# Delta rule in chunks of 64 tokens instead of 128, with products in 64x64 places of the array and the order of work written by hand

## The chip, the cores and the metric

The kernel runs on one core of one Trainium2 chip. The metric is the device time of an execution in microseconds. The kernel before took 1425.95 us (median of 3 runs, 1422.16 to 1428.44).

In the profile PE is TensorE's matmul and PEld its weight load, DVE is VectorE, ACT is ScalarE, POOL is GpSimd, and SP is SyncE, which here issues most DMAs. A matmul of fp32 data leaves two records in the trace.

## What is computed

The first half is a delta rule, for 4 batches, 8 heads, 768 tokens and a head size of 48. The second half is a router with the two best of 8 experts for each of the 3072 tokens, and a mixture of experts with 384 inputs and 1024 hidden units.

```
state = 0                                     # [B, H, 48, 48]
for t in range(768):
    kt = k[t] / (norm(k[t]) + 1e-6)
    y[t]  = q[t] @ state                      # state of before the token
    v_old = kt @ state
    state = state + beta[t] * outer(kt, v[t] - v_old)

x = y as [3072, 384]
noisy = x @ w_gate + log1p(exp(x @ w_noise)) * noise
top2  = the two largest of noisy, softmax over them (+1e-9)
out   = sum over the two: weight * (relu(x @ w1[e]) @ w2[e])
```

## The kernel before

The delta rule goes through the tokens in chunks of C = 128, six of them. In a chunk, each batch is one tile of 128 tokens, with 8 heads in the free dimension, so a chunk is four tiles. Inside a chunk the dependence of tokens on one another is a triangular system, which the kernel solves with an explicit inverse.

`normalize(c)` scales the keys by their norms: squares on ACT, sums and small operations on DVE, a square root on ACT, the multiplication of `kp` on POOL. `products(c)` turns the keys (`turned`: four transposes `p_t` on PE, a copy to `kT` on ACT) and multiplies them with themselves (`gram`: `p_g`, 64-row products in two row places). ACT copies the 32x32 diagonal blocks of the result to `gd` and the rest to `at`. `invert(c)` runs on DVE: it transposes `gd` so that each of 128 partitions holds one 32x32 block (4 batches, 8 heads, 4 blocks), inverts all of them at once in 30 pairs of operations (L326, L330), and transposes back to `tb` (with `beta`) and `w32` (without). `join(c, b)` makes 64x64 inverses `w64` of pairs of them with 32x32 products `p_x` and `p_w`.

`attend(c, b)` is a generator. Its stages are: subtract what the state holds of these keys (`p_b`); the products of queries and keys, masked (`p_g`, `qk`); the upper 64 tokens' update (`solve`: `p_u`, times `beta`); their effect on the lower 64 tokens (`p_e`); the lower update; the new state (`p_s`, added on DVE to the old one in a zero padded layout `st`); the answers `p_y` from state and `qk`; their transposes `p_xt`; the router's logits `p_l`. `run(c)` takes the four batches through these stages in step. `route(c)` computes the noisy logits, the two best experts and the row of each token in its expert's buffer. Two products (`p_at`: `mask_u` with the tokens taken, `ones` with the earlier ones) count the tokens ahead. The rows are then written with indirect DMAs to `rows_x`.

The order of the main loop is `products(c+1)`, `join(c)`, `run(c)`, `route(c)`, `invert(c+1)`, the loads of `k` for chunk c+2, `normalize(c+2)`. All engines take their instructions in the order that the scheduler of the framework makes of this, and each waits by semaphores for the others. All PSUM tiles are of one pool of eight banks. After the delta rule, the mixture goes through the experts: load rows, transpose them (`p_xt`, L604), two products (L611, L620), store. At the end the two rows of each token are gathered and added.

Of the kernel before, what the change touches and what calls it, by code (L numbers as in the profile page):

```python
# [15 lines left out]
C = 128  # L16
DP = 64
Q = 32
# [5 lines left out]
def kernel(  # L24
# [30 lines left out]

    nc = tc.nc
# [6 lines left out]
    NB = C // Q  # L63
    NP = H // 2
    BH = B * H
# [6 lines left out]
    psum = ctx.enter_context(  # L72
        tc.tile_pool(name="psum", bufs=8, space=bass.MemoryType.PSUM)
    )

    def ps(shape, name):
        return psum.tile(shape, FP32, name=name, tag="ps")
# [11 lines left out]
    )  # L89

# [47 lines left out]
    def load_router():  # L138
# [8 lines left out]
        nc.sync.dma_start(  # L147
            out=noise, in_=moe_noise.rearrange("(t p) e -> p t e", p=128)
        )
# [25 lines left out]
    def deltanet(ictx):  # L175

        beta_t = const.tile([128, NCH, BH], FP32, name="beta_t")
        beta_b = const.tile([128, NCH, Q], FP32, name="beta_b")
        with tc.tile_pool(name="setup", bufs=1) as setup:
            beta_sb = setup.tile([BH, S], FP32, name="beta_sb")  # L180
            nc.sync.dma_start(out=beta_sb, in_=beta.rearrange("b h s -> (b h) s"))
            p_bt = ps([128, NCH, BH], "p_bt")
            for c in range(NCH):
                nc.tensor.transpose(
                    p_bt[:, c], beta_sb[:, c * C : (c + 1) * C], ident[0:BH, 0:BH]
                )
            nc.scalar.copy(beta_t, p_bt)
        by_block = beta.rearrange("b h (c n j) -> n (b h) c j", n=NB, j=Q)
        for n in range(NB):
            nc.sync.dma_start(out=beta_b[n * BH : (n + 1) * BH], in_=by_block[n])  # L190

        pool = ictx.enter_context(tc.tile_pool(name="att", bufs=1))

        def sb(shape, name, bufs, tag=None):
            return pool.tile(shape, FP32, name=name, tag=tag or name, bufs=bufs)

        def preset(shape, name, n, where):

            made = []
            for i in range(n):  # L200
# [6 lines left out]
        kps = preset([128, H, DP], "kp", 2 * B, lambda t: [t[:, :, D:DP]])  # L207
        qps = preset([128, H, DP], "qp", B, lambda t: [t[:, :, D:DP]])
        w64s = preset(
            [128, H, 2 * Q], "w64_", 6,  # L210
            lambda t: [t[Q : 2 * Q, :, 0:Q], t[3 * Q :, :, 0:Q]],
        )
        states = [
            preset(
                [128, NP, 2 * D], f"st{b}_", 2,
                lambda t: [t[0:DP, :, D:], t[DP:, :, 0:D]],
            )
            for b in range(B)
        ]

        group = {}
        chunk = {}
        logits = {}
        ys = {}

        def load(c, b, name):
            n = c * B + b
            src = {"k": k, "q": q, "v": v}[name]
            if name == "v":
                to = t = sb([128, H, D], "v", B + 1)  # L230
            else:
                tiles = {"k": kps, "q": qps}[name]
                t = tiles[n % len(tiles)]
                to = t[:, :, 0:D]
            nc.sync.dma_start(
                out=to, in_=src[b, :, c * C : (c + 1) * C, :].rearrange("h p d -> p h d")
            )
            group.setdefault((c, b), {})[name] = t

        def normalize(c):  # L240

            ss = sb([128, BH], "ss", 1)
            for b in range(B):
                ksq = sb([128, H, D], "ksq", 1)
                nc.scalar.activation(ksq, group[c, b]["k"][:, :, 0:D], ACTF.Square)
                nc.vector.tensor_reduce(
                    out=ss[:, b * H : (b + 1) * H], in_=ksq, axis=AX.X, op=ALU.add
                )
            root, rec, ksc = (sb([128, BH], x, 1) for x in ("root", "rec", "ksc"))
            nc.scalar.sqrt(root, ss)  # L250
            nc.vector.tensor_scalar_max(rec, root, 1e-30)
            nc.vector.reciprocal(rec, rec)
# [6 lines left out]
            for b in range(B):  # L259
                kp = group[c, b]["k"]  # L260
                nc.gpsimd.tensor_tensor(  # L261
                    out=kp[:, :, 0:D], in0=kp[:, :, 0:D],
                    in1=ksc[:, b * H : (b + 1) * H, None].to_broadcast([128, H, D]),
# [3 lines left out]
        def turned(src, name, bufs):  # L267

            p_t = ps([128, NP, 128], "p_t")
# [6 lines left out]
        def gram(lhsT, rhs):  # L276

            p_g = [ps([128, NP, 128], f"p_g{par}") for par in range(2)]
            for j in range(NP):
                for par in range(2):  # L280
                    lo = DP * par
                    nc.tensor.matmul(  # L282
                        p_g[par][:, j], lhsT[lo : lo + DP, j], rhs[lo : lo + DP, j]
                    )
            return p_g

        def products(c):
# [4 lines left out]
            gd = chunk[c, "gd"] = sb([128, Q, BH], "gd", 1)  # L292
            for b in range(B):
                g = group[c, b]
                g["kT"] = turned(g["k"], "kT", 2 * B)
                at = g["at"] = sb([128, H, C - Q], "at", 2 * B)
                for par, p in enumerate(gram(g["kT"], g["kT"])):
                    for n in range(NB):
                        rows = slice(n * Q, (n + 1) * Q)
# [71 lines left out]
        def attend(c, b):  # L371
# [15 lines left out]
            if c + 1 < NCH:  # L387
                load(c + 1, b, "q")
# [343 lines left out]
```

## Time and profile before

| | |
|---|---|
| median of 3 runs | 1425.95 us (1422.16 to 1428.44) |
| profiled execution | 1410.04 us, its span 1408.0 us |
| mean granted TensorE clock | 0.779 of full speed |
| PE busy | 1064.6 us (76%) |
| PEld busy | 771.4 us (55%) |
| DVE busy | 393.6 us (28%) |
| ACT busy | 345.3 us (25%) |
| POOL busy | 141.5 us (10%) |
| first product of the mixture | 729.13 us |

The delta rule with the router fills the first 729 us of the span, the mixture with its gather the rest. The shares of the whole span mix both halves, so the first half has to be read in windows. The granted clock is the speed that TensorE was given, as a share of 2.4 GHz: 1.00 is 2.4 GHz, 0.50 is 1.2 GHz. A row of the timeline joins neighbouring instructions of one form; its brackets hold the idle time ahead of them and the engine whose work ended it.

### The profile page before, as it was taken

The numbers are of one execution on the slowest core, as the hardware profiler recorded it, in microseconds if no ns is written. First come the engines' busy times: TensorE is split into PE (matmuls) and PEld (weight loads), VectorE is DVE, ScalarE is ACT, GpSimd is POOL, SyncE is SP. The second block draws the span as 40 slices with busy tenths as digits, with TensorE's granted clock in tenths as the row PEclk, the third lists the DMA queues.
The fourth block names the chain that finished last, engine by engine and source line by source line (L and its number), as shares of the span: only waits on it lengthen the run. The fifth ranks groups of instructions, "written<-read, shape, count | busy, mean of one in ns | idle before, by whom it ended". The sixth has DMA issues, their size and how long they took to land. (4 is left out here: it accounts for less than half of the span.)

```text
span 1408.0 us, 16439 instructions
## 1 busy us (share of the span) xinstructions
PE 1064.6 (76%) x6752; PEld 771.4 (55%) x6752; DVE 393.6 (28%) x1033; ACT 345.3 (25%) x780; POOL 141.5 (10%) x182
## 2 busy tenths in 40 slices
PE   2479259538937937959729999999999999999800
PEld 1369248527927927948725655555555555555400
DVE  1674416605545545533110100101010101010122
ACT  3650551443163164140202020201011110102022
POOL 5000210030040030020010000000000000000075
PEclk9555557756756756756559999999999999999955
DMA  8926924211211211010070122222131312000076
GB/s 219 366 74 188 369 74 126 39 45 24 46 45 24 46 46 22 20 46 1 4 248 33 63 73 79 90 73 95 67 101 61 107 56 73 12 29 6 36 205 198
DMA packets 141043, 124.15 MB, mean 88 GB/s; under 512 B 83072, under 2 KB 133248, under 8 KB 140960
## 3 DMA queue, kind: packets, MB, share of 16 engines
q1 hardware_dynamic: 134816, 104.14, 23.4%
q0 software_dynamic: 6144, 18.88, 4.4%
q8 instruction: 55, 0.90, 0.3%
q14 instruction: 28, 0.23, 0.1%
HBM read 60.09 MB, written 62.91 MB: 87 GB/s over the span
## 5 line engine op out<-in xcount | busy, mean ns | idle before, releaser
L611 PE MATMUL p_h<-xe,w1e 128*128 128x448 f32 x768 | 290.7, 540 | 1.5 <-DVE xe L605 1.5
L620 PE MATMUL p_o<-w2e,hT 128*128 128x384 f32 x896 | 290.3, 486 | 0.0
L620 PEld LDWEIGHTS p_o<-w2e,hT 128*128 128x128 f32 x896 | 170.2, 190 | 119.6 <-issue 3.0
L611 PEld LDWEIGHTS p_h<-xe,w1e 128*128 128x128 f32 x768 | 145.3, 190 | 142.9 <-issue 139.7
L615 ACT ACTIVATE hT<-p_h 128x448 f32<-128x448 f32 x128 | 69.6, 544 | 527.6 <-PE p_h L611 527.6
L624 DVE COPY yr<-p_o 128x384 f32<-128x384 f32 x56 | 31.2, 558 | 543.0 <-PE p_o L620 543.0
L687 POOL DMA_INDIRECT got<-rows_y,slot x48 | 46.8, 975 | 640.6 <-PEq L658 625.6
L282 PE MATMUL p_g<-kT 64*128 64x128 f32 x384 | 49.8, 437 | 67.3 <-ACT kT L273 67.3
L282 PEld LDWEIGHTS p_g<-kT 64*128 64x128 f32 x384 | 42.7, 324 | 76.3 <-ACT kT L273 76.3
L300 ACT COPY gd<-p_g 32x128 f32<-32x128 f32 x192 | 70.2, 365 | 50.7 <-PE p_g L282 49.0
L402 PE MATMUL p_u<-v,w 64*64 64x48 f32 x768 | 69.9, 270 | 0.0
L402 PEld LDWEIGHTS p_u<-v,w 64*64 64x64 f32 x768 | 68.1, 188 | 0.8 <-issue 0.2
L545 PE MATMUL p_at<-r_taken,mask_u 128*128 128x32 f32 x12 | 3.6, 397 | 79.0 <-DVE gate L565 61.7
L330 DVE TENSOR_TENSOR t<-t,step 128x30 f32<-128x30 f32 (+9 forms) x180 | 59.6, 331 | 5.5
L163 POOL DMA_INDIRECT rows_x<-y,slot x48 | 46.6, 971 | 143.5 <-issue 100.6
L271 PE MATMUL p_t<-ident,kp 128*128 128x128 f32 x96 | 26.7, 434 | 44.9 <-POOL kp L261 44.9
L326 DVE TENSOR_TENSOR step<-t 128x30 f32<-128x30 f32 (+9 forms) x180 | 59.2, 329 | 4.9
L453 ACT COPY y<-p_y 128x384 f32<-128x384 f32 x24 | 11.5, 479 | 196.4 <-PE p_y L447 196.4
L447 PE MATMUL p_y<-u,qk 128*128 128x48 f32 x384 | 58.6, 319 | 0.0
L447 PEld LDWEIGHTS p_y<-u,qk 128*128 128x128 f32 x384 | 57.7, 239 | 0.1
L368 PE MATMUL p_w<-w,x 32*32 32x32 f32 x768 | 41.7, 237 | 13.8 <-ACT x L363 13.6
L362 PE MATMUL p_x<-tb,at 32*32 32x32 f32 x768 | 42.8, 237 | 10.4 <-DVE tb L341 6.7
(126 smaller groups left out, 1037.9 us busy)
## 6 DMA issues: line engine op xcount, KB each, us to landing
rows_y<-zero SPq DMA_DIRECT2D x8, 3264.0 KB
w1e<-in_moe_w_dram SPq DMA_DIRECT2D x8, 1536.0 KB
w2e<-in_moe_w_dram SPq DMA_DIRECT2D x8, 1536.0 KB
rows_x<-zero SPq DMA_DIRECT2D x8, 1344.0 KB
xr<-rows_x SPq DMA_DIRECT2D x8, 1344.0 KB
rows_y<-yr SPq DMA_DIRECT2D x56, 192.0 KB
kp<-in_k_dram SPq DMA_DIRECT2D x24, 192.0 KB
qp<-in_q_dram SPq DMA_DIRECT2D x24, 192.0 KB
```

Of the source, the lines that this page charges most:

```text
L163: d = nc.gpsimd.indirect_dma_start(out=rows_x, out_offset=bass.IndirectOffsetOnAxis(ap=slot, axis=0), in_=rows, in_offset=None,).ins
L282: nc.tensor.matmul(p_g[par][:, j], lhsT[lo : lo + DP, j], rhs[lo : lo + DP, j])
L300: nc.scalar.copy(gd[rows].rearrange("p i h -> p h i")[:, b * H + par : (b + 1) * H : 2], p[rows, :, rows],)
L326: nc.vector.tensor_tensor(out=step, in0=t[:, j + 1 :, j, None].to_broadcast(shape), in1=t[:, None, j, 0:j].to_broadcast(shape), op=ALU.mult,)
L330: nc.vector.tensor_tensor(out=t[:, j + 1 :, 0:j], in0=t[:, j + 1 :, 0:j], in1=step, op=ALU.add)
L362: nc.tensor.matmul(p_x[dn, h], at[up, h, up], tb[up, b * H + h])
L402: nc.tensor.matmul(p_u[half, h], w64[half, h], r[half, h])
L447: nc.tensor.matmul(p_y[:, h], qk[:, h], u[:, h], start=(st is None and h == 0), stop=(h == H - 1), skip_group_check=True,)
L611: nc.tensor.matmul(p_h, w1e[:, do, fo * 128 : (fo + 1) * 128], xe[:, do, cols], start=(do == 0), stop=(do == KT - 1),)
L615: nc.scalar.activation(hT[:, fo, cols], p_h, ACTF.Relu)
L620: nc.tensor.matmul(p_o, hT[:, fo, i * 128 : (i + 1) * 128], w2e[:, fo], start=(fo == 0), stop=(fo == FT - 1),)
L687: nc.gpsimd.indirect_dma_start(out=g, out_offset=None, in_=rows_y, in_offset=bass.IndirectOffsetOnAxis(ap=slot[:, n : n + 1], axis=0),)
```

## The change

A chunk is now 64 tokens, twelve of them. A tile holds one chunk of two batches on its 128 partitions (a unit), so a chunk has two units, and four units in two chunks make a step. The block inverses are made for a whole step at once, as before for four tiles, the rest chunk by chunk. Since a 64x64 inverse now covers the chunk, `p_e` and the second `solve` go. `beta` is folded into `w64` by way of `tt`, so `u` is one copy on ACT. Products of keys, queries and states are 64x64, over four quadrants of the array in turns (`by_token`, and `p_s`), each into a tile of two PSUM banks (`banks`, three of them; the rest go to `bank`, two of them). `p_u` and `p_y` use two diagonal quadrants in turns, `p_x` and `p_w` two 32x32 places. A state is added on DVE in one operation to a compact `st`, and POOL copies it to the padded `wide` for `p_y`. The norm's root is an Ln and an Exp, so that ACT keeps one table of functions for the whole stage. Each load of a tile is two DMAs, `k` is loaded three steps ahead, `q` and `v` two chunks ahead, `beta_b` on ACT's queue.

The main loop sets the order by hand. `recur(c)` holds the three stages of the chain (subtract, update, state); between them `take` draws from lists of other work: answers of the chunk before, the router of the step before, products of the step after next, parts of the next step's inverse, query products of the next chunk, and joins of the next step.

```diff
-C = 128
+C = 64
+        def by_token(out, lhsT, rhs, opens=True):
+            for j in range(NP):
+                for b in range(2):
+                    for z in range(2):
+                        nc.tensor.matmul(
+                            out[rows_of[b], z, j], lhsT[rows_of[z], j, rows_of[b]],
+                            rhs(rows_of[z], j, b), start=(j == 0), stop=(j == NP - 1),
+                            skip_group_check=True,
                         )
...
+            p_k = banks(C, "p_k")
+            by_token(p_k, kT, lambda z, j, b: kT[z, j, rows_of[b]])
+            at = g["at"] = sb([128, 2, NP, Q], "at", 3 * US - NU)
+            for b in range(2):
+                for n in range(2):
+                    rows = slice(b * C + n * Q, b * C + (n + 1) * Q)
+                    nc.scalar.copy(gd[rows], p_k[rows, :, :, n * Q : (n + 1) * Q])
+                    if n == 0:
+                        nc.scalar.copy(at[rows], p_k[rows, :, :, Q:C])
...
+            nc.vector.transpose(
+                out=tt.rearrange("p i h -> p (i h)"),
+                in_=scaled.rearrange("p i j -> p (i j)"),
+            )
...
+        def within(n):
+            g = unit[n]
+            qT = g["qT"] = turned(g["q"], "qT", 2 * NU)
+            if n + 2 * NU < NCH * NU:
+                load(n + 2 * NU, "q")
+            yield
+            p_q = banks(C, "p_q")
+            by_token(p_q, g["kT"], lambda z, j, b: qT[z, j, rows_of[b]])
...
+        def recur(c):
+            units = range(c * NU, (c + 1) * NU)
+            for n in units:
+                g = unit[n]
+                st = g["st"] = states.get((c, n % NU))
+                if st is not None:
+                    p_b = banks(D, "p_b")
+                    by_token(p_b, g["kT"], lambda z, j, b: st[z, b, j])
+                    r = by_parity(g["v"])
+                    nc.vector.tensor_tensor(out=r, in0=r, in1=p_b, op=ALU.subtract)
+            yield
...
+                u = g["u"] = sb([128, H, D], "u", 2 * NU + 1)
+                nc.scalar.copy(u, p_u)
...
+                p_s = banks(D, "p_s")
...
+                new = states[c + 1, n % NU] = sb([128, 2, NP, D], f"st{n % NU}", 3)
...
+                    nc.vector.tensor_tensor(out=new, in0=p_s, in1=st, op=ALU.add)
+                wide = wides[n % NU][(c + 1) % 2]
+                for z, rows in enumerate(rows_of):
+                    nc.gpsimd.tensor_copy(wide[rows, :, :, z * D : (z + 1) * D], new[rows])
+            yield
...
+        def take(work, share):
+            for _ in range(share):
+                while work and next(work[0], work) is work:
+                    work.pop(0)
...
         for c in range(NCH):
+            s = c // 2
+            if c % 2 == 0:
+                inverse = [invert(s + 1)] if s + 1 < NS else []
+                take(inverse, 1)
+                if s + 2 < NS:
+                    normalize(s + 2)
+            answers = [answer(n) for n in range((c - 1) * NU, c * NU) if n >= 0]
+            if c % 2 == 0 and c:
+                answers.append(route_later(s - 1))
...
+            for i, _ in enumerate(recur(c)):
+                if i == 0:
+                    take(answers, 3)
+                    if grams:
+                        products(grams[0])
+                    take(inverse, 6)
...
+                else:
+                    take(nexts, 9)
+                    take(answers, 9)
+                    take(inverse, 99 if c % 2 else 5)
+                    if c % 2:
+                        take(joins, 99)
```

The change moves instructions on every engine. The first place is on PE, around the two products `p_at` of a router. Before, they stand between the last logits of a chunk and the transposes of the next keys:

```order
L459 MATMUL p_xt<-ident,y 128x128 x12
L467 MATMUL p_l<-wgn,xT 128x16 x12
L545 MATMUL p_at<-r_taken,mask_u 128x32
L271 MATMUL p_t<-ident,kp_130 128x128 x4
L546 MATMUL p_at<-r_earlier,ones 128x32
```

In the changed kernel they stand in an even chunk, between its updates `p_u` and its states `p_s`:

```order
L485 MATMUL p_u<-v,w_5_163 64x48 x16
L451 MATMUL p_xt<-ident,y 128x128 x3
L459 MATMUL p_xt<-wgn,xT 128x16 x3
L583 MATMUL p_at<-r_taken,mask_u 128x32
L297 MATMUL p_t<-ident,kp_118 128x128 x4
L584 MATMUL p_at<-r_earlier,ones 128x32
L297 MATMUL p_t<-ident,qp_144 128x128 x3
L307 MATMUL p_k<-kT 64x64 x16
L503 MATMUL p_s<-u,kp_124 64x48 x16
L503 MATMUL p_s<-u,kp_126 64x48 x16
```

The logits of the row L459 are written to the spare columns of the tile `p_xt`. The router has moved from the end of a chunk into the middle of the chain of the one after it, ahead of the state's products in the queue.

The second place is on DVE, in the recurrence. Before, pairs of the inversion (`step`, `t`) stand between the operations of four batches:

```order
L391 TENSOR_TENSOR qk<-p_g_1743,mask_u 128x4x128
L403 TENSOR_TENSOR u<-p_u,beta_t 64x384 x2
L326 TENSOR_TENSOR step<-t 128x228
L403 TENSOR_TENSOR u<-p_u,beta_t 64x384 x2
L413 TENSOR_TENSOR v<-v,p_e 64x384 x4
L403 TENSOR_TENSOR u<-p_u,beta_t 64x384 x4
L433 TENSOR_TENSOR st_0_172<-p_s,st_1_175 64x4x48 x2
```

In the changed kernel a step begins, in DVE's queue, with the router's last operations, the even chunk's states, the odd chunk's subtractions and states, and the next inversion's start:

```order
L589 TENSOR_REDUCE r_row<-r_mine 128x4
L590 CAST slot_102<-r_row 128x4
L512 TENSOR_TENSOR st_2080<-p_s,st_1435 128x384
L512 TENSOR_TENSOR st_2101<-p_s,st_1456 128x384
L419 TENSOR_TENSOR qk<-p_q,mask 128x512 x2
L477 TENSOR_TENSOR v<-v,p_b 128x2x4x48 x2
L512 TENSOR_TENSOR st_2446<-p_s,st_2080 128x384
L343 STREAM_TRANSPOSE t<-gd 128x1024
L512 TENSOR_TENSOR st_2467<-p_s,st_2101 128x384
L347 TENSOR_TENSOR t<-t,low_b 128x1024
```

The operations `u` times `beta` and `v` minus `p_e` are gone. The states of an even chunk now stand behind the whole router of the step before, and ahead of that behind the rest of an inversion.

## Rows read from the trace of the kernel before

**Rows 1.** Windows: us, then busy time (count) of each engine, clock, DMA.

```profile
core 0: us, PE busy (x) PEld busy (x) DVE busy (x) ACT busy (x) POOL busy (x), PEclk, DMA share, GB/s
296.20:319.50 23.30, 12.45 (x80) 10.00 (x80) 0.00 (x0) 13.34 (x34) 2.32 (x3) 0.50 0.01 3
319.50:334.30 14.80, 12.10 (x258) 11.85 (x256) 6.95 (x18) 9.31 (x25) 0.00 (x0) 0.50 0.01 2
334.30:386.50 52.20, 49.50 (x502) 47.75 (x500) 30.84 (x72) 8.49 (x21) 0.00 (x0) 0.77 0.23 47
...
729.00:1331.00 602.00, 600.29 (x1834) 336.78 (x1834) 57.52 (x112) 69.64 (x128) 0.00 (x0) 1.00 0.19 65
```

**Rows 2.** Timeline of PE (start us, us, engine, line, operation, tiles), router's end.

```profile
402.03 0.61 PE L545 MATMUL p_at<-r_taken,mask_u 128*128 128x32 f32 x2 [15.51 <-DVE gate L565]
```

**Rows 3.** Timeline of PE, products of each form at their places in the program.

```profile
106.53 6.74 PE L402 MATMUL p_u<-v,w 64*64 64x48 f32 x61
...
126.39 3.65 PE L427 MATMUL p_s<-u,kp 128*64 128x48 f32 x64
...
334.30 7.00 PE L381 MATMUL p_b<-st,kT 128*128 128x96 f32 x32
...
402.45 1.09 PE L271 MATMUL p_t<-ident,kp 128*128 128x128 f32 x4
...
432.29 0.24 PE L368 MATMUL p_w<-w,x 32*32 32x32 f32 x1
...
432.43 1.54 PE L362 MATMUL p_x<-tb,at 32*32 32x32 f32 x29
...
441.24 6.47 PE L381 MATMUL p_b<-st,kT 128*128 128x96 f32 x32
...
687.55 5.14 PE L467 MATMUL p_l<-wgn,xT 128*128 128x16 f32 x24
...
729.13 2.16 PE L604 MATMUL p_xt<-ident,xr 128*128 128x128 f32 x9 [28.66 <-DMA xr<-rows_x]
```

**Rows 4.** Window inside the recurrence, columns as in rows 1.

```profile
356.00:370.00 14.00, 14.00 (x157) 13.91 (x156) 5.52 (x12) 0.00 (x0) 0.00 (x0) 0.50 0.22 44
```

**Rows 5.** Groups by line: shape, count, busy us, mean ns, idle before, releaser.

```profile
L300 ACT COPY gd<-p_g 32x128 f32<-32x128 f32 x192 | 70.2, 365 | 50.7 <-PE p_g L282 49.0
L355 ACT COPY w<-w 32x256 f32<-32x256 f32 x96 | 38.6, 402 | 17.0 <-DVE r_w L493 7.4 <-DVE r_d L506 5.6 <-DVE r_w L505 1.8
...
L246 DVE TENSOR_REDUCE ss<-ksq 128x8 f32<-128x384 f32 x24 | 13.2, 551 | 40.0 <-ACT ksq L245 39.7
```

**Rows 6.** Timeline of DVE: inversions, first state, router with and without POOL.

```profile
48.91 1.25 DVE L317 STREAM_TRANSPOSE t<-gd 128x1024 f32<-128x1024 f32 x1 [3.73 <-ACT gd L300]
...
54.97 0.33 DVE L326 TENSOR_TENSOR step<-t 128x168 f32<-128x168 f32 x1
...
78.18 1.19 DVE L317 STREAM_TRANSPOSE t<-gd 128x1024 f32<-128x1024 f32 x1
...
127.53 3.29 DVE L431 COPY st<-p_s 64x192 f32<-64x192 f32 x8 [0.47 <-PE p_s L427]
...
397.41 2.23 DVE L493 TENSOR_TENSOR r_a_hit<-r_noisy,r_a_top 128x32 f32<-128x32 f32 x1
...
692.93 0.18 DVE L504 TENSOR_SCALAR r_z_pos<-logits 128x32 f32<-128x32 f32 x1 [27.81 <-ACT logits L472]
...
701.69 0.17 DVE L553 CAST slot<-r_row 128x4 int32<-128x4 f32 x1
```

**Rows 7.** Timelines of POOL (key scaling) and of SP (DMA issues).

```profile
21.35 3.19 POOL L261 TENSOR_TENSOR kp<-kp,ksc 128x384 f32<-128x384 f32 x4 [3.19 <-issue]
...
369.00 3.32 SPq L235 DMA_DIRECT2D kp<-in_k_dram  x4
```

**Rows 8.** Timeline of the weight loads, after a key product's turn.

```profile
300.03 0.72 PEld L271 LDWEIGHTS p_t<-ident,kp 128*128 128x128 f32 x4 [0.22 <-issue]
```

More of the change, by code (lines that the diff above doesn't have):

```diff
@@ L89 @@
     )
+    mask = const.tile([128, C], FP32, name="mask")
+    for lo in (0, C):
+        nc.vector.tensor_copy(mask[lo : lo + C], mask_u[lo : lo + C, lo : lo + C])
     low = const.tile([128, Q, Q], FP32, name="low")
@@ L318, in invert @@
                 out=t.rearrange("p i j -> p (i j)"),
[L319 removed]
+                in_=step[s, "gd"].rearrange("p i h -> p (i h)"),
             )
@@ L415, in attend @@
             )
             yield
-            solve(lower)
-            if c + 1 < NCH:
-                load(c + 1, b, "v")
-            yield
-            if c < NCH - 1:
-                p_s = ps([128, NP, D], "p_s")
-                for h in range(H):
-                    to = slice(h % 2 * DP, h % 2 * DP + DP)
-                    nc.tensor.matmul(p_s[to, h // 2], kp[:, h], u[:, h])
-                new = states[b][(c + 1) % 2]
-                for to, cols in ((upper, slice(0, D)), (lower, slice(D, 2 * D))):
-                    if st is None:
-                        nc.vector.tensor_copy(new[to, :, cols], p_s[to])
-                    else:
-                        nc.vector.tensor_tensor(
-                            out=new[to, :, cols], in0=p_s[to], in1=st[to, :, cols],
-                            op=ALU.add,
-                        )
@@ L452, in attend @@
-            y = sb([128, H, D], "y", B + 1)
-            nc.scalar.copy(y, p_y)
-            yield
-            y_f = y.rearrange("p h d -> p (h d)")
-            p_xt = ps([128, KT, 128], "p_xt")
-            for t in range(KT):
-                nc.tensor.transpose(p_xt[:, t], y_f[:, t * 128 : (t + 1) * 128], ident)
-            xT = sb([128, KT, 128], "xT", 2)
-            nc.scalar.copy(xT, p_xt)
-            yield
-            wgn = router["wgn"]
-            p_l = ps([128, 2, E], "p_l")
+            p_l = p_xt[:, KT * 128 : KT * 128 + 2 * E].rearrange("p (x e) -> p x e", e=E)
@@ L466, in attend @@
             for do in range(KT):
                 nc.tensor.matmul(
-                    p_l, xT[:, do], wgn[:, do], start=(do == 0), stop=(do == KT - 1)
-                )
-            if b == 0:
-                logits[c] = sb([128, B, 2, E], "logits", 1)
-            nc.scalar.copy(logits[c][:, b], p_l)
-            ys[c * B + b] = y_f
-        def run(c):
-            todo = [attend(c, b) for b in range(B)]
-            while todo:
-                todo = [a for a in todo if next(a, a) is None]
@@ L573, in deltanet, with now @@
             cleared.append(clear(rows_x, e * N, e * N + TILES * 128))
+        for n in range(2 * US, 3 * US):
+            load(n, "k")
         first_weights = load_weights(w_even, 0)
+        def now(work):
+            for _ in work:
+                pass
         normalize(0)
-        products(0)
-        invert(0)
+        for n in range(US):
+            products(n)
+        now(invert(0))
         normalize(1)
-        for c in range(NCH):
-            if c + 1 < NCH:
-                products(c + 1)
-            for b in range(B):
-                join(c, b)
-            run(c)
-            route(c)
-            if c + 1 < NCH:
-                invert(c + 1)
-            if c + 2 < NCH:
-                for b in range(B):
-                    load(c + 2, b, "k")
-                normalize(c + 2)
+        for n in range(US, 2 * US):
+            products(n)
@@ L592, in deltanet @@
+        now(answer(NU * NCH - 2))
+        now(answer(NU * NCH - 1))
+        route(NS - 1)
         return first_weights
```

438 lines of the change are left out of this document (242 added, 196 removed).

## The prediction, made before the changed kernel was run

> **What bounds the kernel now.** I read the windows first, then PE's timeline with what ended each idle time, then DVE's, then the groups by line. The mixture runs from 729.13 us [rows 3] to the end with PE busy 600.29 of 602 us [rows 1], and the change leaves its code and its data alone. So the gain or loss must come from the 729 us ahead of it. There the period of a chunk of 128 tokens (four tiles) is 441.24 - 334.30 = 107 us, from the first `p_b` of one chunk to that of the next [rows 3]. It has four stretches. The recurrence, 52.2 us, is PE's: busy 49.5 [rows 1]. Then PE waits 15.51 us, because `p_at` of the router stands ahead of everything else in its queue and DVE first ends the inversion and the router [rows 2]. Then the products, about 24 us, are ACT's: in 23.3 us PE is busy 12.45 and DVE not at all [rows 1], while ACT makes the 365 ns copies of L300, 192 of them in all [rows 5]. Last comes the join, 14.8 us, where PE and ACT work on 32x32 pieces [rows 1]. Two engines rest in each stretch while one works, and nothing of the next chunk fills the gap.
>
> **Prices of PE.** An fp32 matmul leaves two records. At the lower clock level (granted 0.50, that is 1.2 GHz) a 64x64 product in one place costs 6.74/61 = 0.110 us a record, and in two places in turn (`p_s`) 3.65/64 = 0.057 [rows 3]. A 32x32 product in one place costs 1.54/29 = 0.053, and where `p_x` and `p_w` alternate between two places five starts lie in 432.43 - 432.29 = 0.14 us, 0.028 each [rows 3]. A turn costs about half for each place added. Four 64x64 places in turn are not in the trace. The floor is the 0.028 of the smaller pair, the ceiling of a gain is no gain over two places, 0.057. I take 0.030, because rows of one family halve twice. A burst of 16 such matmuls (32 records) is then 1.0 us, between 0.9 and 1.8. On the clock: from 356 to 370 us PE is busy 14.00 of 14 us in single-place 64x64 products and the grant is 0.50 [rows 4], so such work does not hold the upper level, and I price all of it at 0.50.
>
> **The change part by part.** A step is now two chunks of 64 tokens, again four tiles; a tile holds 64 tokens of two batches. I follow the two waits that close a step.
>
> Stretch A runs from the first subtraction of `p_b` in an even chunk to the new state of that chunk. By the new order DVE holds there, ahead of that state's add, the rest of one inversion, one normalization and the router of the step before. The inversion's rest took 78.18 - 54.97 = 23.2 us [rows 6]; one of its two transposes now has the plain form that took 1.25 [rows 6], so 22.5. Two subtractions and four reductions of 128x384 at 0.55 [rows 5]: 3.3. Six small operations at 0.18 to 0.35: 1.5. The router alone took 701.69 + 0.17 - 692.93 = 8.9 [rows 6]. One operation of 0.19 stretched to 2.23 beside POOL [rows 6]: 2. After `p_at` the queue of PE holds two sets of transposes, one `p_k` and two `p_s` before the state, about 5.5 us, of which DVE's own slots cover 2: 3 more. A = 41 us. PE's own work there is some 18 us, so its price does not show; the wait of `p_at` stays, with `p_t`, `p_k` and `p_s` queued behind it.
>
> Stretch B, from that state to the next even chunk's subtraction, is PE's. Eleven bursts in four places (four `p_q`, three `p_b`, two `p_k`, two `p_s`): 11.0. Two `p_u` in two diagonal places, 32 records at 0.057: 3.6. Two `p_y`, the same plus 16 records of 96 columns, about 3.1 each: 6.2. Transposes, 5.3 sets at 1.09 less 0.2 of overlap [rows 3]: 4.8. Two `p_xt`, three transposes each instead of four: 1.3. Two of `p_l`, each six records at 5.14/24 = 0.214 [rows 3]: 2.6. The six bursts of `p_x` and `p_w` at 32 x 0.028: 5.3. Sum 34.8, and one to two us of waits for ACT's copies: B = 36. A step is 77 us against 107.
>
> What goes with it at no cost of its own: `p_e` and the second `p_u` (they were in the 52.2 us, and B no longer holds them); the multiplications by `beta`, which are folded into `tt`; the reloads of ACT's tables. ACT has 8.8 us a tile: six copies of `p_k` and four of `tt` of 32x256 at 0.40 [rows 5], and eleven more. Four tiles are 35 us, covered by 77. If that cover were gone (step under 40), ACT would be the bound. POOL gains two copies of a state for each tile, at most 0.9 each (four 128x384 multiplies took 3.19 [rows 7]); only `p_y` reads them, a stage later. SP issues twice as many loads, 24 a step at 3.32/4 = 0.83 [rows 7]: 20 us of 77, asked for one to three steps ahead; past that slack a late `k` would hold up `normalize`. The half loads move the same bytes; their price lies between nothing and those 20 us once, and I take nothing.
>
> The start: the first scaled `k` came at 21.35 [rows 7]; without the transposes of `beta` and the table loads ahead of it I read about 16. The first inversion started at 48.91 [rows 6] after four batches of 32 copies; 24 copies of 0.40 end near 32. Add 29.3 for an inversion (48.91 to 78.18 [rows 6]) and the first `tb` is there near 62 to 65, `p_u` near 82 behind join and `q` products, and the first state near 104 with the second inversion before it on DVE, against 127.53 [rows 6].
>
> The end: after the state of chunk 8 one B without `p_k`, 34; chunk 10 without an inversion, 20; chunk 11 and its answers, 28. From the last `p_l`, 687.55 + 5.14 = 692.69, to the mixture's first `p_xt` at 729.13 is 36.4 [rows 3], and from there to the span's end 1408.0 - 729.13 = 678.9; both stay. Around the span lie 2.0.
>
> Sum: 104 + 4 x 77 - 4 (no normalization in one step) + 34 + 20 + 28 + 36.4 + 678.9 + 2 = 1207. In general 863 + 4A + 5B. The profiled execution took 1410.04, the median of the runs 1425.95, a factor of 1.0113. So 1207 stands for 1221 us; I say 1220.
>
> Where PE went from `p_w` (32x32) to `p_b` (128x128), the new matmuls start at 334.30 [rows 3] with no wait named, and after a transpose's turn the weights' idle time was 0.22 [rows 8]. The Trainium skill, page "TensorEngine Tiling (Array Packing)", section "Key Properties", says that a change of the tiling mode, not of the place alone, drains TensorE. B has some 23 changes of place size: by the rule at 0.22 each, an estimate, 5 us a step and 1246 us in all; by the trace nothing. The measured rows decide for the sum; the other figure lies inside the forecast's own range below and gets no chance apart.
>
> **The rivals.** *B at the upper clock.* The recurrence's mean grant was 0.77, not 0.50 [rows 1], so part of it ran at 2.4 GHz, and denser work could hold that. PE's prices of B would fall by some 30 per cent net of ACT's waits: B = 26, 863 + 164 + 130 = 1157, 1170 us. Against it: the low grant at a full PE [rows 4]. The Trainium skill, page "TensorE: Matmul & The Clock Gate", section "Wait — 56ns, not 53.3ns?", has a gap of about 2.5 ns above the columns' time that the clock does not shorten; no row here separates it.
>
> *Four places give no more than two.* The bursts cost 1.8, eleven of them 9 us more, with waits B = 46: 863 + 164 + 230 = 1257, 1271 us. A longer A of 52, from more POOL interference, gives nearly the same. For it: only pairs have been seen. Against: 0.028 in 32x32.
>
> *The order does not bind.* Engines wait for one another as before and a step stays 107 us: 104 + 428 - 4 + 82 + 717 = 1327, 1342 us. For it: the `p_at` wait is still queued ahead of PE's work.
>
> *Slower: places run one after another.* If four places are done in series at 0.110, a burst is 3.5 instead of 1.0; eleven add 28, `p_u`, `p_y`, `p_x` and `p_w` some 14: B = 78, and start and end gain 35: 863 + 35 + 164 + 390 = 1452, 1468 us. It decides from B = 70 on, which is where 898 + 164 + 5B reaches 1410. Against it: the `p_s` and `p_x`/`p_w` rows.
>
> **How the numbers follow.** Forecast 0.56 (its own range 1185 to 1255), upper clock 0.20, two places 0.15, order not binding 0.05, series 0.04. The runs of the kernel before spread by 0.4 per cent, so 0.5 is about what a measurement can tell from no change. Only the last rival is slower: 0.04. Faster 0.95, the rest 0.01 within. The range takes in the first three and part of the fourth, 1140 to 1295.
>
> **What would show it.** In the changed profile: a step's length, from one even chunk's state to the next, of 77 us; in A, DVE without a gap and PE waiting for DVE at `p_at`; in B, PE busy above nine tenths and DVE mostly waiting for it; a burst `p_q` or `p_b` of 16 matmuls lasting 1.0 us at a grant of 0.50; the first state at 104; the mixture's first `p_xt` near 526 and 679 us from there to the end. I am wrong if a burst takes over 1.8, if ACT, POOL or a load ends PE's long waits, if the grant in B is near 1.0, or if the stretch behind the last `p_l` is not 36.

## The result, and the profile after

The changed kernel takes 1271.53 us (median of four runs, 1264.72 to 1275.98) against 1424.06 us for the kernel before (four runs): a ratio of 0.8938, 95% interval 0.8866 to 0.9009. The forecast was 1220 with a range of 1140 to 1295, so the side and the range hold; the time is 52 us over the forecast and above the forecast's own 1185 to 1255. The profiled execution took 1273.34 us with a span of 1271.6; in its terms the forecast was 1207, and the 66 us between are what has to be found. (The factor of 1.0113 between a profiled execution and the median did not come again, so the medians show the miss 14 us too small.) Every ratio in this document, and every time of the kernel before that stands beside an experiment, leaves out runs that were slower at a lower granted clock.

The first view is DVE's timeline of the changed kernel (start, length, what ended the idle time before). It gives the moments at which the states of chunks 0, 2, 4, 6 and 10 are written, the marks by which the forecast counted, and two waits of the step between.

```profile
125.31 1.02 DVE L510 COPY st<-p_s 128x384 f32<-128x384 f32 x2 [11.30 <-PE p_s L503]
...
209.02 1.02 DVE L512 TENSOR_TENSOR st<-p_s,st 128x384 f32<-128x384 f32 x2 [11.25 <-remote]
...
291.66 0.56 DVE L512 TENSOR_TENSOR st<-p_s,st 128x384 f32<-128x384 f32 x1 [9.78 <-remote]
...
338.33 0.55 DVE L271 TENSOR_REDUCE ss<-ksq 128x8 f32<-128x384 f32 x1 [4.71 <-ACT ksq L270]
...
365.26 0.17 DVE L598 TENSOR_SCALAR gate<-gate 128x4 f32<-128x4 f32 x1 [2.13 <-ACT gate L597]
...
378.59 0.56 DVE L512 TENSOR_TENSOR st<-p_s,st 128x384 f32<-128x384 f32 x1 [9.74 <-remote]
...
502.67 0.56 DVE L512 TENSOR_TENSOR st<-p_s,st 128x384 f32<-128x384 f32 x1 [0.22 <-PE p_s L503]
```

With PE's rows below, the balance against the forecast is (us):

| stretch | forecast | measured | more |
|---|---|---|---|
| start to the first state | 104 | 125.3 | +21 |
| three full steps, chunk 0 to 6 | 231 | 83.7 + 82.6 + 86.9 = 253.3 | +22 |
| chunk 6 to chunk 10 | 73 + 34 + 20 = 127 | 124.1 | -3 |
| chunk 10 to the end of the last `p_l` | 28 | 553.25 - 502.67 = 50.6 | +23 |
| to the mixture's first `p_xt` | 36.4 | 588.45 - 553.25 = 35.2 | -1 |
| from there to the span's end | 678.9 | 1271.6 - 588.45 = 683.2 | +4 |

In each full step DVE stands idle 9.7 to 11.3 us ahead of the state, until `p_s` is there; the sum had 3. PE's timeline shows why; these are its rows in one step, then at the start and at the end. `p_l` has the line's name `p_xt<-wgn,xT` here.

```profile
115.03 1.11 PE L297 MATMUL p_t<-ident,kp 128*128 128x128 f32 x4 [23.71 <-POOL kp L287]
116.08 0.98 PE L485 MATMUL p_u<-v,w 64*64 64x48 f32 x13
...
278.70 0.61 PE L583 MATMUL p_at<-r_taken,mask_u 128*128 128x32 f32 x2 [11.38 <-DVE gate L531]
...
282.08 1.32 PE L503 MATMUL p_s<-u,kp 64*64 64x48 f32 x24
283.64 0.48 PE L503 MATMUL p_s<-u,kp 64*64 64x48 f32 x6 [0.24 <-issue]
284.37 0.49 PE L503 MATMUL p_s<-u,kp 64*64 64x48 f32 x5 [0.24 <-issue]
...
287.29 0.46 PE L503 MATMUL p_s<-u,kp 64*64 64x48 f32 x4 [0.95 <-issue]
288.71 0.47 PE L503 MATMUL p_s<-u,kp 64*64 64x48 f32 x5 [0.96 <-issue]
...
293.25 0.24 PE L503 MATMUL p_s<-u,kp 64*64 64x48 f32 x1 [1.21 <-issue]
293.42 1.75 PE L297 MATMUL p_t<-ident,qp 128*128 128x128 f32 x7
295.10 1.99 PE L307 MATMUL p_q<-qT,kT 64*64 64x64 f32 x64
296.86 1.90 PE L307 MATMUL p_b<-st,kT 64*64 64x48 f32 x64
...
316.23 1.18 PE L307 MATMUL p_q<-qT,kT 64*64 64x64 f32 x64 [1.39 <-ACT qT L299]
...
519.80 0.47 PE L307 MATMUL p_b<-st,kT 64*64 64x48 f32 x4 [0.96 <-issue]
...
551.78 1.47 PE L459 MATMUL p_xt<-wgn,xT 128*128 128x16 f32 x6 [0.62 <-ACT xT L453]
...
588.45 4.49 PE L702 MATMUL p_xt<-ident,xr 128*128 128x128 f32 x21 [27.93 <-DMA xr<-rows_x]
```

The 64 records of `p_q` and of `p_b` run in one piece, 1.99 and 1.90 us. The 64 of `p_s` take from 282.08 to 293.49, in groups of some five with pauses that have no releaser ("issue"). In chunks 8 and 10 it is `p_b` that pauses in this way (the row at 519.80 is one). POOL's timeline has the eight row writes of the step at the same time:

```profile
281.64 1.04 POOL L170 DMA_INDIRECT rows_x<-y,slot  x1 [7.54 <-DVE r_mine L531]
...
290.64 0.97 POOL L170 DMA_INDIRECT rows_x<-y,slot  x1 [0.30 <-issue]
```

The windows (columns as in rows 1) show the full step from chunk 2 to chunk 4, the stretch B behind chunk 4, a burst, and the end from chunk 10 on:

```profile
core 0: us, PE busy (x) PEld busy (x) DVE busy (x) ACT busy (x) POOL busy (x), PEclk, DMA share, GB/s
209.00:291.60 82.60, 53.22 (x1163) 45.85 (x1162) 45.95 (x128) 41.01 (x90) 18.88 (x22) 0.64 0.43 128
...
291.66:323.10 31.44, 25.43 (x758) 22.32 (x760) 12.43 (x26) 16.92 (x39) 4.97 (x8) 0.88 0.69 192
...
295.10:296.80 1.70, 1.70 (x65) 1.70 (x68) 0.50 (x1) 0.59 (x1) 0.14 (x1) 0.50 0.48 96
...
502.70:553.00 50.30, 37.24 (x460) 31.08 (x452) 10.84 (x46) 6.98 (x18) 9.75 (x12) 0.50 0.09 32
```

Last, the groups by line (count, busy us, mean ns, idle before) that answer to [rows 5]:

```profile
L387 ACT COPY w<-tt 32x256 f32<-32x256 f32 x96 | 60.1, 626 | 9.5 <-DVE tt L369 8.2
L330 ACT COPY gd<-p_k 32x256 f32<-32x256 f32 x96 | 56.3, 586 | 25.0 <-PE p_k L307 14.4 <-remote 6.1 <-PE p_s L503 3.6
L503 PE MATMUL p_s<-u,kp 64*64 64x48 f32 x704 | 30.8, 284 | 15.2 <-issue 15.1
```

### The profile page after: what moved, and what is told of

It is laid out like the page before. It is cut to its first block, busy times and chain, and to the rows that moved or that the text cites. A ratio compares the mean times of both kernels' runs of the same rounds, so it can differ in the third digit from the quotient of the medians.

```text
span 1271.6 us, 20241 instructions
## 1 busy us (share of the span) xinstructions
PE 936.2 (74%) x8634; PEld 628.1 (49%) x8634; DVE 341.6 (27%) x923; ACT 332.5 (26%) x693; POOL 168.7 (13%) x222
## 5 line engine op out<-in xcount | busy, mean ns | idle before, releaser
L353 DVE TENSOR_TENSOR part<-t 128x30 f32<-128x30 f32 (+9 forms) x180 | 64.1, 356 | 4.7
L357 DVE TENSOR_TENSOR t<-t,part 128x30 f32<-128x30 f32 (+9 forms) x180 | 63.8, 354 | 4.8
L330 ACT COPY gd<-p_k 32x256 f32<-32x256 f32 x96 | 56.3, 586 | 25.0 <-PE p_k L307 14.4
L387 ACT COPY w<-tt 32x256 f32<-32x256 f32 x96 | 60.1, 626 | 9.5 <-DVE tt L369 8.2
L515 POOL COPY wide<-st 64x384 f32<-64x384 f32 x44 | 26.3, 599 | 172.2 <-DVE st L512 136.2
L702 PE MATMUL p_xt<-ident,xr 128*128 128x128 f32 x168 | 21.7, 290 | 27.9 <-DMA xr<-rows_x 27.9
L503 PE MATMUL p_s<-u,kp 64*64 64x48 f32 x704 | 30.8, 284 | 15.2 <-issue 15.1
L440 PE MATMUL p_y<-u,qk 64*64 64x48 f32 x768 | 40.2, 274 | 0.0
L307 PE MATMUL p_b<-st,kT 64*64 64x48 f32 x704 | 31.2, 283 | 12.0 <-issue 11.9
L440 PEld LDWEIGHTS p_y<-u,qk 64*64 64x64 f32 x768 | 36.5, 189 | 4.5 <-issue 3.7
```

Of the source, the lines that this page charges most:

```text
L307: nc.tensor.matmul(out[rows_of[b], z, j], lhsT[rows_of[z], j, rows_of[b]], rhs(rows_of[z], j, b), start=(j == 0), stop=(j == NP - 1), skip ...
L330: nc.scalar.copy(gd[rows], p_k[rows, :, :, n * Q : (n + 1) * Q])
L353: nc.vector.tensor_tensor(out=part, in0=t[:, j + 1 :, j, None].to_broadcast(shape), in1=t[:, None, j, 0:j].to_broadcast(shape), op=ALU.mult,)
L357: nc.vector.tensor_tensor(out=t[:, j + 1 :, 0:j], in0=t[:, j + 1 :, 0:j], in1=part, op=ALU.add)
L387: nc.scalar.copy(w64[rows, :, cols], tt[rows])
L440: nc.tensor.matmul(p_y[b, h], qk[b, h % 2, h // 2], u[b, h], start=(c == 0 and h == 0), stop=(h == H - 1), skip_group_check=True,)
```

## Experiments

Ratios are against the kernel before, measured beside the experiment on the same chip. Experiments 1 to 4 ran on one chip (kernel before 1407.55 us), 5 to 8 on a second (1413.74), 9 to 11 on a third (1397.00) and 12 on a fourth (1398.04); the two pairs turned out to differ in the pauses.

**1. Places one after another.** In `by_token` and in the loops of `p_s` the place becomes the outer loop:

```diff
-for j in range(NP):
-    for b in range(2):
-        for z in range(2):
+for b in range(2):
+    for z in range(2):
+        for j in range(NP):
```

> The 64x64 products p_k, p_q, p_b and p_s do the four of one place after another instead of going round the four places; nothing else changes. Theory (the gain of these products comes from places overlapping in turns): a burst of 32 records rises from about 1.0 us to 3.5 us at a grant of 0.50, as the one-place products of the kernel before at 0.110 us a record; 92 bursts in all, of which those beside DVE's inversion cost nothing, so 100 to 190 us more than the changed kernel, 1370 to 1460 us. Rival (a burst is bound by the supply of instructions or by weight loads, not by the place): within 20 us of 1272.

Measured 1336.64 us, ratio 0.9477 (0.9412 to 0.9542): 65 us more than the changed kernel, 76 by the ratios, and less than the 100 to 190 expected. Taking places in turns is a part of the gain, but a smaller one than was priced. The rest of the 152 us gained belongs to the shorter chunk and the order by hand, and no run takes these two apart. Sixty-one records of `p_q` took 3.83 us, 0.063 each:

```profile
333.46 3.83 PE L307 MATMUL p_q<-qT,kT 64*64 64x64 f32 x61
```

That is twice the 0.031 in turns, not the 0.110 of the single place before [rows 3]. The grant was 0.58 from 333.4 to 337.3 us, which accounts for a part; the rest is open.

**2. No row writes** (but for the last step's):

```diff
 for slot in slots:
-    spread(ys[n], slot[:, n : n + 1])
+    if s == NS - 1:
+        spread(ys[n], slot[:, n : n + 1])
```

> The rows of the first five steps are not written to rows_x (that part of the computation is left out; the last step's rows are written). Theory (PE's stalls of 0.25 to 1.2 us between groups of four to six products in the even chunks are caused by the eight indirect row writes that run at that time): the stalls go, the p_s of an even chunk take 2 us instead of 9 to 11, and the first p_xt of the mixture comes 30 to 40 us earlier, at about 550 to 558 instead of 588; time about 1235. Rival (the stalls belong to these products' place in the program, or to other transfers): the gaps stay and the time is 1265 to 1275.

Measured 1215.71 us in one run, which has no interval, beyond either figure. PE's timeline has the same `p_s` in one piece, and the windows of the last chunks have another clock:

```profile
278.89 1.91 PE L503 MATMUL p_s<-u,kp 64*64 64x48 f32 x64
```

```profile
core 0: us, PE busy (x) PEld busy (x) DVE busy (x) ACT busy (x) POOL busy (x), PEclk, DMA share, GB/s
...
460.60:497.00 36.40, 23.61 (x460) 20.10 (x452) 13.60 (x62) 8.06 (x23) 2.01 (x4) 0.76 0.01 1
```

The states of chunks 0, 6 and 10 come at 125.42, 356.41 and 460.62 us, the last `p_l` ends at 493.24 and `p_xt` starts at 528.86. So the three steps lose 253.3 - 231.0 = 22 us, chunks 6 to 10 lose 20, the end loses 50.6 - 32.6 = 18: 60 us in all, with the start unchanged. These two profiles are not of one chip; experiment 4, on the chip of this run and with the pauses in its `p_s`, took 47 us more than this run. At the end the grant was 0.76 here and 0.50 with the writes.

**3. Products behind the state.** The set of `products` (with `p_t<-ident,kp`) moves from the first half of a step to the second:

```diff
-if grams:
-    products(grams[0])
...
 take(answers, 9)
+for n in grams:
+    products(n)
```

> The key products of the step after next stand behind the state's products of the chunk in the written order, not ahead of its updates. Theory (PE's queue position: the transposes of kp wait for normalize on DVE and POOL, and p_u is queued behind them): the first state comes near 101 us instead of 125, and PE's waits for kp of 4.7, 6.1 and 8.4 us in the steps go; at least 24 us and up to 60 less, 1210 to 1247. Rival (DVE's serial work of about 40 us sets the step wherever PE's products stand): only the start gains, the steps stay at 83 to 87 us, 1245 to 1252.

Measured 1264.57 us, ratio 0.8975 (0.8898 to 0.9052): no difference from the changed kernel, and beyond either figure. The first state came at 93.62 us instead of 125.31, so the 23.71 us wait for POOL was the start's cost. But from chunk 0 to chunk 10 it took 77.3 + 84.7 + 81.5 + 81.3 + 74.6 = 399.4 us instead of 377.4: the inversion ends later, and DVE has it ahead of the odd chunk's subtraction, which then still waits for PE:

```profile
290.36 0.56 DVE L477 TENSOR_TENSOR v<-v,p_b 128x384 f32<-128x384 f32 x1 [2.77 <-PE p_b L307]
```

The inversion's last transpose stands ahead of it from 285.57 us on, and its `p_b` starts only at 289.24 on PE, behind the moved `p_k`, which now pause beside the row writes (273.0 to 282.9). Of the 31.7 us that the early start gained, 22.0 were given back by chunk 10.

**4. Inversion held** behind the chain's last DVE operation, by an added dependence:

```diff
-nc.vector.tensor_tensor(
+behind(nc.vector.tensor_tensor(
     out=part, in0=t[:, j + 1 :, j, None].to_broadcast(shape),
```

> Each part of the next step's inversion is tied behind the last subtraction or state of the chain that the program's text puts ahead of it, so that DVE cannot run ahead with it; key products stay where they are. Theory (DVE's order costs: the scheduler gathers all 30 pairs of an inversion in the even chunk ahead of the state): 13 to 20 us of the pairs move into the odd chunk where DVE waited for PE, each full step falls from 84 to about 68, time 1205 to 1235. Rival (PE's queue: p_u waits for normalize behind the transposes of kp, so the pairs only change places with other waits): within 15 us of 1272.

Measured 1262.99 us, ratio 0.8956 (0.8881 to 0.9031): no change, as the rival had it. The pairs did move: 12 stand between subtraction and state where the changed kernel has 24. The first state came at 106.41 us, 19 earlier, and 11 of these were given back by chunk 10 (388.4 us for 377.4). DVE's order alone is not what lengthens a step.

**5. Rows written a step late**, behind the even chunk's subtraction, with two more buffers for `y`:

```diff
-for n in range(s * US, (s + 1) * US):
-    for slot in slots:
-        spread(ys[n], slot[:, n : n + 1])
...
+if c % 2 == 0 and s >= 2:
+    write_rows(s - 2)
```

> The eight indirect row writes of a step are issued one step later, in the next even chunk behind its subtractions, where PE waits for DVE's inversion and for kp; all rows are still written. Theory (row writes cost by stalling PE's products that run at that time, and nothing where PE waits anyway): the stalls leave p_s and p_b, and most of the 58 us that went without the writes comes back: 1215 to 1240 us. Rival (the cost is POOL's time: its scaling of kp and its state copies stand behind the writes in its queue): the writes now stand ahead of kp's scaling, each of three full steps stays at 83 to 90 us, 1260 to 1280 us.

Measured 1250.65 us, ratio 0.8832 (0.8796 to 0.8869): a small gain at most, as the intervals just touch, and outside both figures. On PE's timeline `p_s` is whole again, and the pauses have gone with the writes to the products that now run beside them:

```profile
362.25 1.90 PE L507 MATMUL p_s<-u,kp 64*64 64x48 f32 x64
...
509.17 0.32 PE L489 MATMUL p_u<-v,w 64*64 64x48 f32 x4 [1.10 <-issue]
512.03 0.46 PE L489 MATMUL p_u<-v,w 64*64 64x48 f32 x4 [1.10 <-issue]
```

Experiment 8, on the same chip and with the writes where the changed kernel has them, has the pauses in `p_s`:

```profile
292.45 0.48 PE L503 MATMUL p_s<-u,kp 64*64 64x48 f32 x5 [0.96 <-issue]
```

So on this chip the pauses follow the writes and not the instruction. Joined with experiment 3 and with experiment 4, this version gave no more:

**6. Held, rows late, products late** (the edits of 3, 4 and 5).

> Three moves together: the inversion's parts tied to the chain's stages (as in the run with the inversion held), key products behind the state, and row writes in the next even chunk. Theory (three waits are in parallel in the chain, and taking away one leaves the next one): what none of the first two did alone shows when all are taken away; first state near 94 us, a step of 62 to 70 us, time 1160 to 1195. Rival (DVE's total work and its router ahead of the odd subtraction set the step): steps of 75 us and over, 1200 to 1235.

**7. Products late, rows late** (the edits of 3 and 5).

> Key products behind the state, and row writes in the next even chunk; the inversion is left to the scheduler. Theory (the gains of the start, 32 us, and of the stalls, 58 us, add, less the 20 that the last steps gave back): 1185 to 1210. Rival (DVE's inversion ahead of the odd subtraction takes what the writes give): 1225 to 1250.

Measured 1257.12 (0.8861 to 0.8928) and 1252.74 (0.8824 to 0.8888). Both theories that gave the order of the step the rest of the loss fell, and both rivals had lower times too (1200 to 1235, and 1225 to 1250).

**8. One store for each tile** of the output instead of two halves:

```diff
-for i in range(2):
-    t0 = (2 * u + i) * S + c * C
-    nc.sync.dma_start(out=out[t0 : t0 + C, :], in_=got[0][i * C : i * C + C])
+rows = out.rearrange("(u i s) d -> u i s d", i=2, s=S)[u, :, c * C : (c + 1) * C]
+nc.sync.dma_start(out=rows, in_=got[0])
```

> The output of a tile is stored with one DMA of 128 rows again, not with two of 64. Theory (the gather at the end, 81.5 us from the last product to the span's end instead of 77.1, pays for 24 more issues on SP): 4 us less, 1266 to 1269. Rival (the difference is the gather's own spread from run to run): within 1.5 us of the changed kernel.

Measured 1317.95 us, ratio 0.9317 (0.9286 to 0.9348): some 50 us slower, the opposite of what was expected. In SP's queue the 24 stores to three-dimensional views take 109.14 us from the first to the last, and the 48 half stores of the changed kernel 66.90:

```profile
1204.10 109.14 SPq L797 DMA_DIRECT2D out_dram<-got  x24
```

```profile
1201.36 66.90 SPq L798 DMA_DIRECT2D out_dram<-got  x48
```

The gathers on POOL tell why. They wait 52.3 us, in 18 waits, for a store to land and free its tile (us in total, times, longest); in the changed kernel it is 0.6 us:

```profile
POOL got L783 <- DMA out_dram<-got: 52.3, 18, 4.9
```

While one of these stores is under way (1268.99 to 1271.2 us) SP's queue keeps 13.5% of the 16 DMA engines busy, which is about two of them; with the half stores it is 60.7% (1241 to 1243 us). So this form of store is slow in itself, and the run says nothing of what 24 fewer issues are worth: the 4 us of the last stretch stay open.

**9. Rows in PE's waits.** Each step's writes go behind `scaled` of a later inversion, the last ones behind `z_pos` of the next router, where PE waits for DVE:

```diff
+if s >= 3:
+    write_rows(s - 3, made)
...
+if s >= NS - 2:
+    write_rows(s - 1, first)
```

> The eight row writes of a step are issued where PE waits: behind the last multiplication of the inversion in an even chunk (three steps), behind the first operation of the next router (two steps); all rows are written. Theory (the writes cost through stalls of PE at that time and through the clock that PE loses by them): p_s and p_b of the even chunks without stalls, steps of 74 to 79 us instead of 83 to 87, the mixture's first p_xt near 545 to 560 and the time 1228 to 1245. Rival (the writes' cost is the transfers themselves wherever they lie, as the 1251 us of the run with rows written late suggests): 1246 to 1256.

**10. Square root again**: the writes stay where the changed kernel has them, only the norm is computed with `sqrt`, which brings the table loads back.

```diff
-nc.scalar.activation(root, root, ACTF.Ln)
-nc.scalar.activation(root, root, ACTF.Exp, scale=0.5)
+nc.scalar.sqrt(root, ss)
```

> The norm's root is a square root of ACT again, with its tables reloaded between it and the router's functions, in place of Ln and Exp with one table. Forecast's theory (ACT has 35 us of work in a step of 84 and hides the reloads): within 6 us of the changed kernel, 1266 to 1278. Rival (the reloads stand in the chain from the norm to kp, p_t and p_u, and in the router ahead of p_at): 2.6 to 5 us for each of six steps, 1287 to 1302.

**11. Rows in waits, products late** (the edits of 9 and 3).

> Row writes in the waits as in the run of that name, and key products behind the state's. Theory (start and stalls are separate costs and add): first state near 94 us and no stalls in p_s and p_b; 1215 to 1235. Rival (DVE's serial work takes back what the start gives, as with the products alone): within 6 us of the run with the rows in waits.

Measured 1217.01 (ratio 0.8691 to 0.8791), 1221.64 (0.8668 to 0.8769) and 1208.89 (0.8656; 0.861 to 0.8702). All three lie below both figures expected of them. Taken alone, 9 looks like the cure. But 10 left the writes where they were and has 24 table loads where the changed kernel has one, and it too is far below 0.8938. In its timelines of POOL and PE, `p_s` is whole while the eight writes of its step run:

```profile
207.61 1.19 POOL L170 DMA_INDIRECT rows_x<-y,slot  x1 [6.94 <-DVE r_mine L530]
...
216.71 0.96 POOL L170 DMA_INDIRECT rows_x<-y,slot  x1 [0.31 <-issue]
```

```profile
209.62 1.90 PE L502 MATMUL p_s<-u,kp 64*64 64x48 f32 x64
```

**12. Both places in one kernel**: steps 0 and 1 write where the changed kernel does, the later ones as in 9 (the diff is against 9).

```diff
-if s >= 3:
+if s == 5:
     write_rows(s - 3, made)
...
-if s == NS - 1:
+if s in (0, 1, NS - 1):
     write_rows(s)
```

> Row writes of the first two steps stay where the changed kernel has them (even chunks of the second and third step, beside the states' products), those of the next three are issued in the waits, as in the run with the rows in waits; all rows are written. In the last three runs the kernel before took 1397 us, not 1416 to 1424, and the run with the square root showed no stalls although its writes lie where the changed kernel has them. Theory A (the stalls belong to the place of the writes alone): p_s of the second and third step take 9 to 11 us each, none of the later products stalls, about 1232 to 1245 us where the kernel before takes 1397 to 1424. Theory B (the stalls need the writes and a condition outside the kernel that changed between the runs): where the kernel before takes near 1397 us, no stalls at either place and 1210 to 1222 us; where it takes 1416 or more, stalls in the second and third step and few behind, 1235 to 1255.

Measured 1214.26 us, ratio 0.8697 (0.866 to 0.8734), as theory B had it. On a fourth chip, and at the old place of the writes, `p_s` is again whole beside them:

```profile
278.67 1.90 PE L506 MATMUL p_s<-u,kp 64*64 64x48 f32 x64
```

```profile
278.22 1.04 POOL L170 DMA_INDIRECT rows_x<-y,slot  x1 [7.54 <-DVE r_mine L542]
...
287.21 0.97 POOL L170 DMA_INDIRECT rows_x<-y,slot  x1 [0.30 <-issue]
```

So the pauses need the row writes (2, and 5 where they moved) and something outside the kernel that two of the four chips had and two had not. Each chip was measured at another time, so the chip and the hour are not told apart. The gain of 9 is therefore not shown to come from its edit. The changed kernel itself wasn't run on the chips without pauses; 10, nearest to it, stood at 0.8719 there. The best version measured is 11; its interval overlaps those of 9, 10 and 12.

## Why the prediction was right, and where its sum was off

**The range.** It holds, but partly by luck. Start, steps and end each missed by 21 to 23 us in the same direction, and the range was wide because it took in the rivals. The time is even the 1271 of the rival "four places give no more than two", which the price of a burst refutes. Beside that rival the prediction named a longer A of 52 us from POOL's interference: A was 52.7 on the mean of three steps, for another reason.

**The bound.** Right: the mixture kept its 602 us (588.45 to 1190.1), and all of the gain came ahead of it. The stretch behind the last `p_l` was 35.2 us for 36.4.

**The price of a burst.** Right, and it carried the forecast: 1.99 us for 64 records is 0.031 each, 0.030 was taken, at a grant of 0.50. Two diagonal places cost 1.95/32 = 0.061 for `p_y`, where 0.057 stood. Beside the row writes it does not hold (64 records of `p_s` in 11.4 us, well over the 1.8 a burst that was to show the prediction wrong). The rival "four places give no more than two" is out by the undisturbed rows, and "places run one after another" by experiment 1. The latter's own price was too high (0.063 measured for 0.110), and so was its time.

**A change of place size costs nothing.** Right here: in the rows above `p_t` in 128x128 runs into `p_q` in 64x64 (293.42 + 1.75 = 295.17, next start 295.10), with no idle time. The Trainium skill, page "TensorEngine Tiling (Array Packing)", section "Key Properties", has TensorE drained at a change of mode; no such gap shows. The ends of matmuls are modelled, so a drain of less than some 0.1 us could hide. The 0.22 us of [rows 8] stand ahead of transposes and behind a key product, not behind a transpose as the prediction reads it.

**Costs put at nothing.** The loads held: from 80 us to the mixture none ended a wait of over 0.3 us. ACT's cover held in its sum, although the copies took 586 and 626 ns and not 0.40 us: ACT was busy 41.01 us of a step's 82.60, where 35 were priced. A single copy was priced from rows of other access patterns [rows 5]. It did not hold in its order: in the step at chunk 6 DVE waits 4.71 us for ACT's squares and 2.13 us for the exponential of a gate, which stands in ACT's queue behind eight copies of `tt`. Both waits lie in stretch A.

**Stretch A is the step that was mis-sized.** Forecast A was 41 us; in the three full steps it was 49.6, 53.1 and 55.5. Take the last, from the subtraction at 323.10 us to the state at 378.59. Two terms make the 14. The inversion and normalization ended at 356.97, 33.9 us instead of 27.3: DVE waited 4.71 us for ACT's squares, and four operations beside POOL's scaling of `k` took 0.84 to 1.02 us where their neighbours took 0.3. The router's rest up to `p_at` took the 8.7 us that were left for it (8.9, and 2 for an operation beside POOL, less the 2 of DVE's slots behind `p_at`), although the 2.13 us wait for ACT is in it. And "about 5.5 us" of PE's queue between `p_at` and the state became 378.59 - 365.67 = 12.9. That last term is the one that failed: the transposes and `p_k` were in the sum, but the two `p_s` were given their bare price, and beside the row writes they take 9 to 11 us, a wait that the profile puts down to nothing it shows. In experiment 2 the same stretch is 356.41 - 351.91 = 4.5 us, and A 44.3 on the mean. The prediction looked for POOL's contention on DVE and missed that the same eight transfers could hold up PE. The trace of the kernel before has seven such pauses (us in total, times, longest), beside the row writes of its fifth chunk, and none beside its other five:

```profile
PE p_x L362 <- issue: 3.7, 7, 1.0
```

Experiment 2 prices the writes at 47 us (against experiment 4) to 60 us (profile against profile) over the whole recurrence; the sum had nothing for them.

**Stretch B.** It was given 36 us and took 34.1, 29.6 and 31.4 (323.10 - 291.66) in the full steps, so the step's error is A's alone. The rival "B at the upper clock" is largely true, and pricing all of B at 0.50 failed: the grant was 0.64 over a step but 0.80, 0.85 and 0.88 in these stretches, and a burst at a grant of 1.00 took 1.18 us for 64 records, 0.018 each. B did not fall to that rival's 26, as PE was busy 79 to 89% of it and not above nine tenths. The gain of 4 us a step in B hides a part of the loss in A.

**The start.** Failed by 21 us. The prediction saw that `p_t<-ident,kp` stands in PE's queue ahead of work that others wait for, and it did not apply this to the start: `p_u` of chunk 0 stands behind the `p_t` of the third set, which waits 23.71 us for POOL's scaled `k`, which waits for DVE's norm behind the second inversion. That POOL ends a long wait of PE was one of the prediction's signs of being wrong. Experiment 3 removed that row and the state came 32 us earlier.

**The end.** It was given 28 us and took 50.6. Experiment 2 puts 18 of the 23 on the row writes, with the clock: all of the stretch was granted 0.50 with the writes, and 0.76 without. Whether the pauses lower the clock or the clock makes them long isn't told apart.

**A balance inside.** Chunks 6 to 10 came out right (124.1 for 127) by two errors: without a normalization the state of chunk 8 comes ahead of the rest of the inversion, 49.6 us after chunk 6 instead of 73, and what it had not waited for follows, 74.5 us instead of 54. The total agrees by luck: without the writes (experiment 2) these chunks take 104.2 us, so the sum was 23 us too high for them and the pauses filled most of that.

## What to carry to other kernels

Price a stretch of short products by what else runs in it, and list its DMA bursts, even where they use no operand of it. In an in-order queue look at the first pass through the loop too: what stands ahead there may wait for work that a later pass already has. And before a gain is put down to an edit, run the unedited kernel on the same chip: nearly the same kernel stood at 0.8938 and, on another chip, at 0.8719, which is more than any edit gained that kept the whole computation.

## What the runs showed of the hardware

The pauses were not expected, and their mechanism stays open. In the DMA view of the changed kernel from 281 to 292 us the row writes are the only queue at work (packets, MB, share of 16 engines):

```profile
q0 software_dynamic: 448, 1.38, 33.7%
```

In experiment 10 from 207 to 218 us, where `p_s` does not pause, loads and instructions are fetched beside them:

```profile
q0 software_dynamic: 429, 1.34, 32.8%
q1 hardware_dynamic: 2553, 0.48, 22.5%
q8 instruction: 2, 0.03, 1.2%
```

So the pauses are not a matter of how busy the DMA engines are, and no fetch of instructions was under way while `p_s` paused. The pauses recur about every 0.7 or 1.4 us (starts at 283.64, 284.37, 287.29, 288.71).
